# Top-k attention and a gated feed-forward on one core: score halves in one op, last keys of P.V in column halves, a retuned order

## The chip, the cores and the metric

One core of one Trainium2 chip runs the whole program in one launch. The metric is device microseconds (us) of an execution. The engines are called as the profile calls them: PE (TensorE, with PEld for its weight loads), DVE (VectorE), ACT (ScalarE), POOL (GpSimd) and SP (SyncE, which issues the DMAs). PE's clock has two levels here, 1.2 and 2.4 GHz; the profile gives the granted share of the higher one.

## What is computed

```python
def _attn_ref(q, k, v):                       # q, k, v: (4, 8, 576, 64)
    scores = scale * np.matmul(q, k.transpose(0, 1, 3, 2))
    kth = np.partition(scores, -32, axis=-1)[..., -32:-31]
    scores = np.where(scores >= kth, scores, -1e9)
    attn = np.exp(scores - np.max(scores, axis=-1, keepdims=True))
    attn = attn / (np.sum(attn, axis=-1, keepdims=True) + 1e-09)
    return np.matmul(attn, v)

def _moe_ref(x, w_gate, w_val, w_out, rms_g): # x: (2304, 512), 1536 hidden
    rms = np.sqrt(np.mean(x * x, axis=-1, keepdims=True) + 1e-06)
    xn = x / rms * rms_g
    g = xn @ w_gate
    silu = g * (1.0 / (1.0 + np.exp(-g)))
    return silu * (xn @ w_val) @ w_out
```

The three weights arrive as 64-bit floats; the kernel cuts them down on the chip.

## The kernel before

**Attention** goes in 72 steps. A step handles two heads (`e` = 0, 1) for 128 queries. Its scores (128 x 576 for each head) come in two key halves of 288. Each half is one PE op of six matmuls: `qh·kh`, `ql·kh` and `qh·kl` (values split into a high and a low part), each for both heads, with 64 rows of the array for each head (L513 to L525). An op writes two PSUM banks, one for each head. ACT copies each bank into the slot `sp` (L528). DVE then finds the 32nd largest score: minimum and maximum of the two halves (L501, L502, which read half 0 straight from its bank and half 1 from `sp`), one MAX8 over the minima (L503), and four MAX8 (L506) with three MATCH_REPLACE8 between them (L508). POOL makes the thresholds (L535), ACT and POOL mask, ACT takes the exponential (L539 to L541), PE transposes the nine 128-key blocks (L564), ACT copies them to `pt` and `ptt` (L566), and PE multiplies with `v` (P.V, L575 to L580). In P.V the head's 512 first keys go in matmuls on 64 columns of the array, one column half for each head, side by side; the 64 last keys of both heads go ahead of them in one matmul on all 128 columns (`ptt`, `vt[:, 512:640]`).

**The feed-forward** comes in units: after 256 tokens (after 128 at the start), their output is transposed and normalised (L624 to L665), then each of 12 blocks m (six in a 128-token unit) runs 24 gate and value matmuls into one bank (L697 to L706), ACT's tanh (L708), products on POOL (L711, L712) or on DVE (L714), the product with the value half (L715), a split, and the output matmuls (`wo`, L731 to L736).

**The weights** are read in the first part: 36 pieces (12 each of `w_gate`, `w_val`, `w_out`), each a DMA of 512 KB into one of two raw buffers. A piece is cut down in three DVE instructions (L356 to L358), or, where `PR["HV"]` has the weight's bit, at half its value in two DVE instructions, an ACT Sign and a POOL add (L351 to L354). A POOL subtraction makes the low part of either (L362).

**The order** of every engine's instructions is written by a planner, `_Plan`: each op has an engine, a duration, a priority (`pri`, with offsets from the table `PR`) and its PSUM banks. `place` walks through time, takes for a free engine the ready op of the best priority whose banks are free, and the ops are emitted by their planned start. On the chip each engine then follows that fixed order and waits with semaphores. Banks belong to groups: four in `a` (scores, transposes, P.V, weights), two in `g` (gates), two in `o` (outputs). The key `("turn", 0)` keeps a half-0 score op behind L502 of the step before.

Of the kernel before, what the change touches and what calls it, by code (L numbers as in the profile page):

```python
# [34 lines left out]
)  # L35

# [14 lines left out]
class _Plan:  # L51
# [10 lines left out]
    def add(self, eng, dur, fn, r=(), w=(), bank=None, pri=0.0, nbytes=0, sh=False):  # L62
        o = _Op()
        banks = () if bank is None else bank if isinstance(bank, tuple) else (bank,)
        o.eng, o.dur, o.fn, o.pri, o.banks, o.nbytes, o.sh = eng, dur, fn, pri, banks, nbytes, sh
        o.succ, o.pred = [], []
        deps = {}
        for key in r:
            p = self.writer.get(key)
            if p is not None:  # L70
                deps[id(p)] = (p, True)
            self.readers.setdefault(key, []).append(o)
        for key in w:
            for x in self.readers.get(key, ()):
                if x is not o:
                    deps.setdefault(id(x), (x, False))
            p = self.writer.get(key)
            if p is not None:
                deps[id(p)] = (p, True)
            self.writer[key] = o  # L80
            self.readers[key] = []
        for b in banks:
            if b.last is None:
                b.first = o
            else:
                deps.setdefault(id(b.last), (b.last, False))
            b.last = o
        for p, raw in deps.values():
            p.succ.append((len(self.ops), raw))
            o.pred.append((p.index, raw))  # L90
        o.index = len(self.ops)
        self.ops.append(o)
        return o

    def place(self, key, back=False):
# [14 lines left out]
        busy, win, warm = {}, 0, False  # L110
# [4 lines left out]
        while left:  # L115
            for e in range(5):
# [109 lines left out]
def tile_topk_attention_moe(  # L226
# [30 lines left out]
    NS, NK, NV, NQ, NPT, NWO, NQR = 4, 4, 2, 3, 3, 2, 2  # L257
# [4 lines left out]
    krawt = sb("krawt", [64, 2, 2, D])  # L262
# [45 lines left out]
    def build(exact):  # L308


        plan = _Plan({"a": banks[0:4], "g": banks[4:6], "o": banks[6:8]})
# [82 lines left out]
        def prep_k(b, pair, pri):  # L394
# [4 lines left out]
            dma(krawt[:, g], k[b, h0:h0 + 2, 512:576].rearrange("h s d -> s h d"), 32768, (), (("krawt", g),), pri - 2)  # L399
# [3 lines left out]
            tail = _Bank("a")  # L403
            add(PE, 0.12, lambda: nc.tensor.transpose(tail.tile[:, 0:64], krawt[:, g].rearrange("p h d -> p (h d)"), ident[0:64, 0:64]), r=(("krawt", g),), w=(("kh", s, 1), ("kl", s, 1)), bank=tail, pri=ko)
            ends = [t[s].rearrange("p (n c) -> p n c", c=64)[:, 0:10:9, :] for t in (kh, kl)]

            def twice():
                return tail.tile[:, 0:64].unsqueeze(1).to_broadcast([128, 2, 64])
            add(ACT, 0.19, lambda: nc.scalar.copy(ends[0], twice()), w=(("kh", s, 1),), bank=tail, pri=ko)
            add(DVE, 0.2, lambda: nc.vector.tensor_tensor(ends[1], twice(), ends[0].bitcast(F32), op=ALU.subtract), r=(("kh", s, 1),), w=(("kl", s, 1),), bank=tail, pri=ko)  # L410
# [10 lines left out]
        def vkeys(s):  # L421
            return ("vt", s, 0), ("vt", s, 1)
# [59 lines left out]
        def topk(i, e, bank, pri):  # L482
# [18 lines left out]
            add(DVE, 0.365, lambda: nc.vector.tensor_tensor(mn[:, e, :], bank.tile[:, 0:half], b, op=ALU.min), r=bk, w=(nk,), bank=bank, pri=pri)  # L501
            add(DVE, 0.365, lambda: nc.vector.tensor_tensor(row[:, 0:half], bank.tile[:, 0:half], b, op=ALU.max), r=bk + (("turn", 0),), w=(mk,), bank=bank, pri=pri)  # L502
            add(DVE, 0.385, lambda: nc.vector.max(row[:, half:half + 8], mn[:, e, :]), r=(nk,), w=(mk,), pri=pri)  # L503
            for n in range(4):
                o8 = row[:, rounds[n]]
                add(DVE, 0.388, lambda o8=o8: nc.vector.max(o8, row[:, 0:half + 8]), w=(mk,), pri=pri + 0.1 * n)  # L506
                if n < 3:
                    add(DVE, 0.446, lambda o8=o8: nc.vector.match_replace(row[:, 0:half + 8], o8, row[:, 0:half + 8], NEG), w=(mk,), pri=pri + 0.1 * n)  # L508

        def attend(i, cols, qs, sums, pri):  # L510
# [3 lines left out]
            for half in (1, 0):  # L514
                bank = tuple(_Bank("a") for e in range(2))

                def sm(bank=bank, half=half):
                    terms = [(col, pair, qq, kk) for pair, col in cols for qq, kk in ((qh, kh), (ql, kh), (qh, kl))]
# [51 lines left out]
        def attend_out(i, j, pair, vs, pri):  # L570
# [4 lines left out]
            def pv():  # L575
                mm(bank.tile[:, 0:128], vv[:, 512:640], pc, True, False)
# [3 lines left out]
            add(PE, 1.3, pv, r=(ck, ak, bk) + vkeys(vs), w=(("xv", j, pair),), bank=bank, pri=pri)  # L580
            add(ACT, 0.245, lambda: nc.scalar.copy(xv[:, pair, j * 128:(j + 1) * 128], bank.tile[:, 0:128]), w=(("xv", j, pair),), bank=bank, pri=pri + PR["EV"])

        def attend_out_tail(i, b, half, vs, rslot, pri):
# [21 lines left out]
            add(PE, 1.64, pv, r=(ck, ak, bk) + vkeys(vs[0]) + vkeys(vs[1]), w=(("xvt", 0), ("xvt", 1)), bank=bank, pri=pri)  # L605
# [8 lines left out]
        def feed_forward(u, js, xs, xkeys, rslot, stores, pri, last=False):  # L614
# [57 lines left out]
            for m in range(FC // per):  # L672
# [19 lines left out]
                gb = _Bank("g")  # L692
# [187 lines left out]
```

## Time and profile before

| | |
|---|---|
| median of 3 runs | 917.86 us (914.8 to 918.97) |
| profiled execution, its own time | 917.72 us |
| its span, first to last instruction | 915.8 us |
| mean granted PE clock | 0.955 |

The span is what the profile sees; the run's time is 1.9 us longer. "Busy" of an engine is the union of its instructions' records, which overlap in the pipelines; how long an instruction holds its engine is seen better in the distance between two starts.

### The profile page before, as it was taken

To read this page: it belongs to the slowest core of one execution; us is meant where nothing else is said; L and a number is where in the kernel's file an instruction comes from. 1 tells how busy PE (TensorE), PEld (TensorE's weight loads), DVE (VectorE), ACT (ScalarE), POOL (GpSimd) and SP (SyncE) were. 2 spreads that over 40 slices of the span, in tenths; PEclk is the share of its full clock that TensorE was granted. 3 is DMA by queue.
4 is the path that set the end of the run, shared out by engine and by line. 5 is a ranking of instruction groups with operands and counts; after the bars stand their busy time and mean duration, and the time that the engine had idled before them with its cause. 6 is when DMAs were issued, how large, how long until landed. Compare 5 with 4: busy or idle time off the path is not lost.

```text
span 915.8 us, 19289 instructions
## 1 busy us (share of the span) xinstructions
PE 837.1 (91%) x6618; PEld 714.5 (78%) x6618; DVE 727.7 (79%) x2272; ACT 621.7 (68%) x1549; POOL 517.8 (57%) x742
## 2 busy tenths in 40 slices
PE   5578776799899989999999989999999999999996
PEld 3456555678788858888888778889888988889995
DVE  5999998987798899965999889866898869694211
ACT  5766766787677887776778777766687667755311
POOL 6458998957665555667557544474653444434211
PEclk9976977999999999999999989999999999999999
DMA  9143675454643232224333313145332242332432
GB/s 242 53 137 109 214 229 207 155 175 132 193 121 99 97 93 79 100 83 133 125 100 106 125 61 112 47 135 170 102 115 89 88 158 99 96 110 80 132 134 97
DMA packets 86651, 112.89 MB, mean 123 GB/s; under 512 B 50832, under 2 KB 64144, under 8 KB 86544
## 3 DMA queue, kind: packets, MB, share of 16 engines
q1 hardware_dynamic: 86544, 111.57, 38.6%
q8 instruction: 54, 0.88, 0.4%
q14 instruction: 53, 0.43, 0.2%
HBM read 100.53 MB, written 11.01 MB: 122 GB/s over the span
## 4 chain that ended last, share of the span: by engine, by line
PE 75%; DVE 11%; DMA 5%; ACT 4%; POOL 2%; issue 1%; SPq 0%; POOLq 0%; DVEq 0%; ACTq 0%
PE bank L315 65%; PE bank L564 7%; DVE mx L506 3%; DVE mx L508 3%; DMA kraw<-in_moe_w_val_dram 2%; DMA kraw<-in_moe_w_out_dram 1%; PE bank L443 1%; ACT rr L539 1%; DVE mn L501 1%; PE bank L415 1%; PE bank L624 1%; DVE mx L502 1%; PE bank L659 1%; DVE mx L503 1%; ACT sp L541 1%
## 5 line engine op out<-in xcount | busy, mean ns | idle before, releaser
L506 DVE MAX8 mx<-mx 128x8 f32<-128x296 f32 x576 | 241.6, 455 | 0.0
L540 POOL TENSOR_TENSOR sp<-sp,rr 128x576 f32<-128x576 f32 x144 | 183.9, 1289 | 76.6 <-ACT rr L539 71.1
L508 DVE MATCH_REPLACE8 mx<-mx 128x296 f32<-128x296 f32 x432 | 191.9, 451 | 0.0
L315 PE MATMUL bank<-wo,hh 128*128 128x512 f32 x432 | 149.0, 426 | 3.3 <-DMA wo<-wosc 1.4
L727 POOL TENSOR_TENSOR hl<-tg,hh 128x256 fp32r<-128x256 f32 x108 | 79.4, 737 | 116.9 <-ACT hh L726 102.4
L564 PE MATMUL bank<-ident,sp 128*128 128x128 f32 x648 | 108.6, 293 | 26.5 <-ACT sp L541 6.2
L528 ACT COPY sp<-bank 128x288 f32<-128x288 f32 x288 | 101.2, 405 | 36.6 <-PE bank L315 34.7
L541 ACT ACTIVATE sp<-sp,bt 128x576 f32<-128x576 f32 x144 | 112.7, 783 | 11.7 <-POOL sp L540 11.3
L539 ACT ACTIVATE rr<-sp,bt 128x576 bf16<-128x576 f32 x144 | 108.0, 779 | 12.2 <-POOL bt L535 12.1
L315 PE MATMUL bank<-xth,wgh 128*128 128x256 f32 x384 | 116.3, 303 | 0.0
L564 PEld LDWEIGHTS bank<-ident,sp 128*128 128x128 f32 x648 | 79.6, 148 | 46.7 <-ACT sp L541 7.6
L315 PE MATMUL bank<-xth,wvh 128*128 128x256 f32 x384 | 112.4, 293 | 0.0
L566 ACT COPY pt<-bank 128x512 f32<-128x512 f32 x144 | 84.7, 590 | 37.7 <-PE bank L564 33.7
L315 PE MATMUL bank<-xtl,wgh 128*128 128x256 f32 x384 | 107.7, 281 | 0.0
L315 PE MATMUL bank<-xth,wgl 128*128 128x256 f32 x384 | 107.7, 280 | 0.0
L315 PE MATMUL bank<-xth,wvl 128*128 128x256 f32 x384 | 107.3, 279 | 0.0
L315 PE MATMUL bank<-xtl,wvh 128*128 128x256 f32 x384 | 107.2, 279 | 0.0
L708 ACT ACTIVATE tg<-bank 128x256 f32<-128x256 f32 x108 | 41.5, 385 | 78.7 <-PE bank L315 77.2
L714 DVE SCALAR_TENSOR_TENSOR tg<-tg,bank 128x256 f32<-128x256 f32 x76 | 31.6, 415 | 74.8 <-ACT tg L708 74.3
L501 DVE TENSOR_TENSOR mn<-bank,sp 128x288 f32<-128x288 f32 x144 | 60.7, 448 | 35.7 <-ACT sp L528 35.3
L315 PE MATMUL bank<-kh,qh 64*128 64x288 f32 x320 | 73.5, 396 | 15.5 <-DVE mx L502 5.1
L315 PE MATMUL bank<-wo,hl 128*128 128x512 f32 x216 | 86.6, 401 | 0.2
(151 smaller groups left out, 2076.2 us busy)
## 6 DMA issues: line engine op xcount, KB each, us to landing
wo<-wosc SPq DMA_DIRECT2D x108, 512.0 KB, 3.3
vt<-in_v_dram SPq DMA_DIRECT2D x52, 256.0 KB, 3.0
xvt<-in_moe_w_gate_dram SPq DMA_DIRECT2D x12, 512.0 KB, 4.2
wosc<-wo SPq DMA_DIRECT2D x12, 512.0 KB, 3.6
kraw<-in_k_dram SPq DMA_DIRECT2D x32, 128.0 KB, 3.2
kraw<-in_moe_w_val_dram SPq DMA_DIRECT2D x8, 512.0 KB, 3.8
qraw<-in_q_dram SPq DMA_DIRECT2D x56, 64.0 KB, 2.4
out_dram<-osb SPq DMA_DIRECT2D x14, 256.0 KB, 2.4
```

The lines of the kernel that those rows point to most:

```text
L315: nc.tensor.matmul(o, l, r, start=start, stop=stop)
L501: add(DVE, 0.365, lambda: nc.vector.tensor_tensor(mn[:, e, :], bank.tile[:, 0:half], b, op=ALU.min), r=bk, w=(nk,), bank=bank, pri=pri)
L506: add(DVE, 0.388, lambda o8=o8: nc.vector.max(o8, row[:, 0:half + 8]), w=(mk,), pri=pri + 0.1 * n)
L508: add(DVE, 0.446, lambda o8=o8: nc.vector.match_replace(row[:, 0:half + 8], o8, row[:, 0:half + 8], NEG), w=(mk,), pri=pri + 0.1 * n)
L528: add(ACT, 0.32, lambda b=bank[e], c0=c0: nc.scalar.copy(sp[s][:, c0:c0 + 288], b.tile[:, 0:288]), w=(("sp", s, e, half),), bank=bank[e], ...
L539: add(ACT, 0.7, lambda e=e, tl=tl: nc.scalar.activation(rr[e], tl, AF.Relu, bias=bt[t][:, e, 2:3], scale=-BIG), r=(("bt", t),) + spkeys(i, ...
L540: add(POOL, 1.27, lambda e=e, tl=tl: nc.gpsimd.tensor_tensor(tl, tl, rr[e], op=ALU.subtract), r=(("rr", e),), w=spkeys(i, e), pri=pri + PR ...
L541: add(ACT, 0.8, lambda e=e, tl=tl: nc.scalar.activation(tl, tl, AF.Exp, bias=bt[t][:, e, 1:2], scale=SCALE, accum_out=sums(e)[0]), r=(("bt ...
L564: nc.tensor.transpose(bank.tile[:, c * 128:(c + 1) * 128], sp[s][:, c0 + c * 128:c0 + (c + 1) * 128], ident)
L566: add(ACT, 0.228 if n == 1 else 0.507, lambda dst=dst, bank=bank, n=n: nc.scalar.copy(dst[:, 0:n * 128], bank.tile[:, 0:n * 128]), w=(key, ...
L708: add(ACT, 0.325, lambda gb=gb, hs=hs: nc.scalar.activation(th[hs], gb.tile[:, 0:256], AF.Tanh, scale=1.0 if halves[0] else 0.5), w=(("th" ...
L727: add(POOL, 0.75, lambda hs=hs: nc.gpsimd.tensor_tensor(hl[hs], th[hs], hh[hs].bitcast(F32), op=ALU.subtract), r=(("th", hs), ("hh", hs)), ...
```

## The change

- Both score halves of both heads become one PE op of 12 matmuls and four banks; the `turn` key now holds for the whole op.
- The last keys in P.V go in two column halves, so that a P.V op has one tile shape from its first matmul to its last.
- The transposes of the last 64 keys of K are made for two pairs at once, on the whole array.
- The gates' bank group is dissolved: `a` has six banks.
- The planner adds `SWITCH` to a PE op whose mode (1: row halves, 2: column halves, 0: the rest) differs from that of the op before.
- `sp` has five slots for four, `pt` four for three.
- `HV` 6 to 7: `w_gate`'s twelve pieces go the way of L351 to L354 too. `Z0` 2 to 0: no block takes the POOL way of L710 to L712 any more, all take L714.
- The other numbers of `PR` and some planned durations change.

```diff
-    HV=6, SU=1, ZU=5, F1=2, FX0=-3, FS0=0.5, FD0=-2, Z0=2, QN=0, FE=-8, EV=-1, SO=-2.5, WP1=0.5, WI=-4, FO=-0.5, FS=0.8, ZP=0, KO=-3, WP0=1, FB=3.5, AO=-0.9, FX=-30, QO=-3, TB=0.1, WO=-4, SM=0,
+    HV=7, SU=1, ZU=6, F1=5.02, FX0=-3.08, FS0=0.39, FD0=-2.4, Z0=0, QN=0, FE=-9.01, EV=-2.13, SO=-2.7, WP1=0.21, WI=-6.69, FO=2.17, FS=0.8, ZP=0, KO=-4.26, WP0=1.0, FB=3.5, AO=0.79, FX=-16.28, QO=-3, TB=0.35, WO=-1.76, SM=1.12,
+SWITCH = 0.2
...
+                    if o.mode != mode:
+                        dur, mode = dur + SWITCH, o.mode
...
-    NS, NK, NV, NQ, NPT, NWO, NQR = 4, 4, 2, 3, 3, 2, 2
+    NS, NK, NV, NQ, NPT, NWO, NQR = 5, 4, 2, 3, 4, 2, 2
...
-        plan = _Plan({"a": banks[0:4], "g": banks[4:6], "o": banks[6:8]})
+        plan = _Plan({"a": banks[0:6], "o": banks[6:8]})
...
+            if g == 0:
...
+                add(PE, 0.11, lambda: nc.tensor.transpose(tail.tile[:, 0:128], krawt.rearrange("p h d -> p (h d)"), ident), r=(("krawt", 0), ("krawt", 1)), w=tuple((n, t, 1) for n in ("kh", "kl") for t in two), bank=tail, pri=ko)
...
-            for half in (1, 0):
-                bank = tuple(_Bank("a") for e in range(2))
...
+            bank = {(half, e): _Bank("a") for half in (1, 0) for e in range(2)}
...
+            def sm():
+                for half in (1, 0):
                     for n, (col, pair, qq, kk) in enumerate(terms):
                         for e in range(2):
                             es = slice(64 * e, 64 * e + 64)
                             c0 = 64 * (1 - e) + half * 288
-                            mm(bank[e].tile[:, 0:288], qq[qs][es, col, :], kk[pair % NK][es, c0:c0 + 288], n == 0, n == len(terms) - 1)
...
+                            mm(bank[half, e].tile[:, 0:288], qq[qs][es, col, :], kk[pair % NK][es, c0:c0 + 288], n == 0, n == len(terms) - 1)
+            kk = tuple((n, pair % NK, z) for n in ("kh", "kl") for pair, _ in cols for z in range(2))
+            add(PE, 0.8 * len(cols), sm, r=(("qh", qs), ("ql", qs)) + kk, w=spkeys(i, 0, 1) + ((("turn", 0),) if not exact else ()), bank=tuple(bank.values()), pri=pri + PR["SO"], mode=1)
...
             def pv():
-                mm(bank.tile[:, 0:128], vv[:, 512:640], pc, True, False)
+                for e in range(2):
+                    mm(bank.tile[64 * e:64 * e + 64, 0:128], vv[:, 512 + 64 * e:576 + 64 * e], pc, True, False)
...
-                gb = _Bank("g")
+                gb = _Bank("a")
```

PE in the feed-forward of a 256-token unit, with the scores of attention step 41 (`kh`, `kl`, `qh`, `ql`) between gate matmuls (`xth`, `xtl` with `wgh`, `wgl`). Before, the first half of that step's scores:

```order
L315 MATMUL bank_68<-xth,wgl 128x256
L315 MATMUL bank_65<-kh_79,qh_94 128x288
L315 MATMUL bank_66<-kh_79,qh_94 128x288
L315 MATMUL bank_65<-kh_79,ql_97 128x288
L315 MATMUL bank_66<-kh_79,ql_97 128x288
L315 MATMUL bank_65<-kl_83,qh_94 128x288
L315 MATMUL bank_66<-kl_83,qh_94 128x288
L315 MATMUL bank_68<-xth,wgh 128x256
L315 MATMUL bank_68<-xtl,wgh 128x256
```

The same step's scores on PE in the changed kernel:

```order
L321 MATMUL bank_64<-kh_79,qh_94 128x288
L321 MATMUL bank_66<-kh_79,qh_94 128x288
L321 MATMUL bank_64<-kh_79,ql_97 128x288
L321 MATMUL bank_66<-kh_79,ql_97 128x288
L321 MATMUL bank_64<-kl_83,qh_94 128x288
L321 MATMUL bank_66<-kl_83,qh_94 128x288
L321 MATMUL bank_67<-kh_79,qh_94 128x288
L321 MATMUL bank_65<-kh_79,qh_94 128x288
L321 MATMUL bank_67<-kh_79,ql_97 128x288
L321 MATMUL bank_65<-kh_79,ql_97 128x288
L321 MATMUL bank_67<-kl_83,qh_94 128x288
L321 MATMUL bank_65<-kl_83,qh_94 128x288
```

Before, four more gate matmuls and then the second half follow these rows; now the halves stand together, with a gate block of 24 matmuls behind them.

PE at the first P.V of the program, before (`ptt` holds the last keys of both heads, `pt` the others):

```order
L564 MATMUL bank_66<-ident,sp_98 128x128 x9
L315 MATMUL bank_66<-ptt_118,vt_87 128x128
L315 MATMUL bank_66<-pt_115,vt_87 64x128
L315 MATMUL bank_66<-pt_116,vt_87 64x128
L315 MATMUL bank_66<-pt_115,vt_87 64x128
```

And in the changed kernel:

```order
L575 MATMUL bank_64<-ident,sp_98 128x128 x4
L575 MATMUL bank_67<-ident,sp_98 128x128
L575 MATMUL bank_68<-ident,sp_98 128x128 x4
L321 MATMUL bank_67<-ptt_120,vt_87 64x128 x2
L321 MATMUL bank_67<-pt_118,vt_87 64x128
```

One matmul on 128 columns has become two on 64; the tile shape still changes once ahead of the P.V and once behind it.

DVE at the start of the program, before (`kl` is the low part of the last keys of K, `xvt` and `tg` raw weights):

```order
L356 TENSOR_SCALAR bank_63<-xvt 128x512
L357 SCALAR_TENSOR_TENSOR bank_63<-xvt,bank_63 128x512
L358 SCALAR_TENSOR_TENSOR x_120<-xvt,bank_63 128x512
L351 TENSOR_SCALAR bank_65<-tg 128x512
L352 SCALAR_TENSOR_TENSOR osb<-tg,bank_65 128x512
L410 TENSOR_TENSOR kl_83<-bank_64,kh_79 128x2x64
```

And in the changed kernel:

```order
L420 TENSOR_TENSOR kl_83<-bank_64,kh_79 128x2x64
L420 TENSOR_TENSOR kl_84<-bank_64,kh_80 128x2x64
L357 TENSOR_SCALAR bank_66<-xvt 128x512
L358 SCALAR_TENSOR_TENSOR x_122<-xvt,bank_66 128x512
L357 TENSOR_SCALAR bank_65<-tg 128x512
L358 SCALAR_TENSOR_TENSOR osb<-tg,bank_65 128x512
L511 TENSOR_TENSOR mn<-bank_63,sp_98 128x288
```

K comes ahead of the weights now, a piece of `w_gate` takes two instructions in place of three, and the first step's search starts behind two pieces; before, four pieces stand ahead of it.

## Rows read from the trace of the kernel before

**Rows 1.** The page: busy time of each engine; the chain that ended last.

```profile
PE 837.1 (91%) x6618; PEld 714.5 (78%) x6618; DVE 727.7 (79%) x2272; ACT 621.7 (68%) x1549; POOL 517.8 (57%) x742
...
PE 75%; DVE 11%; DMA 5%; ACT 4%; POOL 2%; issue 1%; SPq 0%; POOLq 0%; DVEq 0%; ACTq 0%
```

**Rows 2.** Windows: length, busy PE, PEld, DVE, ACT, POOL, then clock, DMA.

```profile
100.00:125.00 25.00, 15.71 (x102) 11.96 (x101) 23.43 (x59) 18.06 (x42) 22.91 (x24) 0.91 0.78 247
...
0.00:175.00 175.00, 119.73 (x672) 88.78 (x673) 156.66 (x427) 119.46 (x276) 130.21 (x165) 0.81 0.55 173
175.00:321.00 146.00, 141.43 (x1230) 121.64 (x1229) 125.38 (x416) 113.40 (x296) 95.17 (x133) 1.00 0.43 133
321.00:346.00 25.00, 19.85 (x129) 14.12 (x127) 24.84 (x82) 20.74 (x53) 14.56 (x30) 0.93 0.32 100
...
519.00:540.00 21.00, 15.01 (x87) 11.70 (x87) 19.82 (x64) 17.34 (x43) 12.70 (x27) 0.76 0.33 108
540.00:854.00 314.00, 313.81 (x2657) 278.42 (x2656) 244.27 (x785) 209.37 (x524) 148.86 (x228) 1.00 0.33 104
854.00:916.00 62.00, 54.38 (x377) 49.39 (x375) 11.78 (x28) 12.71 (x30) 9.56 (x13) 0.97 0.38 129
```

**Rows 3.** Timeline of PE around half a step's scores: start, duration, instruction.

```profile
429.15 0.28 PE L315 MATMUL bank<-xth,wgl 128*128 128x256 f32 x1
429.36 0.40 PE L315 MATMUL bank<-kh,qh 64*128 64x288 f32 x2
429.60 0.29 PE L315 MATMUL bank<-kh,ql 64*128 64x288 f32 x2
429.73 0.29 PE L315 MATMUL bank<-kl,qh 64*128 64x288 f32 x2
429.96 0.39 PE L315 MATMUL bank<-xth,wgh 128*128 128x256 f32 x1
430.19 0.28 PE L315 MATMUL bank<-xtl,wgh 128*128 128x256 f32 x1
430.30 0.28 PE L315 MATMUL bank<-xth,wgl 128*128 128x256 f32 x1
```

**Rows 4.** Timeline of PE at a P.V and the transposes behind it.

```profile
395.15 0.38 PE L315 MATMUL bank<-ptt,vt 128*128 128x128 f32 x2
395.47 1.09 PE L315 MATMUL bank<-pt,vt 128*64 128x128 f32 x16
396.49 1.20 PE L564 MATMUL bank<-ident,sp 128*128 128x128 f32 x9
```

**Rows 5.** Groups of instructions by line and form: count, busy us, mean ns, idle before.

```profile
L315 PEld LDWEIGHTS bank<-pt,vt 128*64 128x64 f32 x1280 | 68.9, 145 | 9.3 <-issue 1.8
...
L714 DVE SCALAR_TENSOR_TENSOR tg<-tg,bank 128x256 f32<-128x256 f32 x76 | 31.6, 415 | 74.8 <-ACT tg L708 74.3
...
L712 POOL TENSOR_TENSOR tg<-tg 128x256 f32<-128x256 f32 x32 | 23.6, 736 | 1.1
...
L357 DVE SCALAR_TENSOR_TENSOR bank<-xvt,bank 128x512 uint32<-128x512 uint32 x12 | 8.3, 695 | 0.3
...
L354 POOL TENSOR_TENSOR x<-x,wo 128x512 int32<-128x512 int32 x5 | 6.5, 1291 | 0.0
```

**Rows 6.** The same view of DVE's first 175 us: two of these to a step.

```profile
L503 DVE MAX8 mx<-mn 128x8 f32<-128x288 f32 x26 | 11.0, 449 | 0.0
```

**Rows 7.** The waits: who waited for whom, us, times, longest.

```profile
DVE mn L501 <- ACT sp L528: 35.3, 23, 6.1
```

**Rows 8.** What the engine waited for ahead of instructions with K: us, times.

```profile
  DVE mx L502: 12.2, 13
```

**Rows 9.** The chain that ended last, at the start: start, us.

```profile
3.23 5.20 DMA kraw<-in_k_dram
8.56 1.10 PE bank L415 x4
```

**Rows 10.** Timeline of DVE: the first instruction of the first search.

```profile
18.58 0.46 DVE L501 TENSOR_TENSOR mn<-bank,sp 128x288 f32<-128x288 f32 x1 [2.27 <-ACT sp L528]
```

More of the change, by code (lines that the diff above doesn't have):

```diff
@@ L60, in __init__, with add @@
         self.bank_tail = {}
-    def add(self, eng, dur, fn, r=(), w=(), bank=None, pri=0.0, nbytes=0, sh=False):
+    def add(self, eng, dur, fn, r=(), w=(), bank=None, pri=0.0, nbytes=0, sh=False, mode=0):
         o = _Op()
         banks = () if bank is None else bank if isinstance(bank, tuple) else (bank,)
-        o.eng, o.dur, o.fn, o.pri, o.banks, o.nbytes, o.sh = eng, dur, fn, pri, banks, nbytes, sh
+        o.eng, o.dur, o.fn, o.pri, o.banks, o.nbytes, o.sh, o.mode = eng, dur, fn, pri, banks, nbytes, sh, mode
         o.succ, o.pred = [], []
@@ L109, in place @@
         dma_free = t = 0.0
-        busy, win, warm = {}, 0, False
+        busy, win, warm, mode = {}, 0, False, 0
         left = len(ops)
@@ L261, in tile_topk_attention_moe @@
     kraw = sb("kraw", [128, 2, 4, 2, D])
-    krawt = sb("krawt", [64, 2, 2, D])
+    krawt = sb("krawt", [128, 2, D])
     kh = [sb(f"kh{i}", [128, S + 64], F32R) for i in range(NK)]
@@ L402, in prep_k, with twice @@
             ko = pri + PR["KO"]
[L403 to L410, printed above, removed]
+            if g == 0:
+                for y in range(2):
+                    dma(krawt[64 * y:64 * y + 64], k[b, h0 + 2 * y:h0 + 2 * y + 2, 512:576].rearrange("h s d -> s h d"), 32768, (), (("krawt", y),), pri - 2)
+                tail = _Bank("a")
+                two = (s, s + 1)
+                add(PE, 0.11, lambda: nc.tensor.transpose(tail.tile[:, 0:128], krawt.rearrange("p h d -> p (h d)"), ident), r=(("krawt", 0), ("krawt", 1)), w=tuple((n, t, 1) for n in ("kh", "kl") for t in two), bank=tail, pri=ko)
+                for y, t in enumerate(two):
+                    ends = [n[t].rearrange("p (n c) -> p n c", c=64)[:, 0:10:9, :] for n in (kh, kl)]
+                    def twice(y=y):
+                        return tail.tile[:, 64 * y:64 * y + 64].unsqueeze(1).to_broadcast([128, 2, 64])
+                    add(ACT, 0.19, lambda ends=ends, twice=twice: nc.scalar.copy(ends[0], twice()), w=(("kh", t, 1),), bank=tail, pri=ko)
+                    add(DVE, 0.25, lambda ends=ends, twice=twice: nc.vector.tensor_tensor(ends[1], twice(), ends[0].bitcast(F32), op=ALU.subtract), r=(("kh", t, 1),), w=(("kl", t, 1),), bank=tail, pri=ko)
             bank, z = _Bank("a"), slot()
@@ L522, in sm @@
                             c0 = 64 * (1 - e) + half * 288
-                            mm(bank[e].tile[:, 0:288], qq[qs][es, col, :], kk[pair % NK][es, c0:c0 + 288], n == 0, n == len(terms) - 1)
-                kk = tuple((n, pair % NK, z) for n in ("kh", "kl") for pair, _ in cols for z in range(2))
-                add(PE, 0.42 * len(cols), sm, r=(("qh", qs), ("ql", qs)) + kk, w=tuple(("sp", s, e, half) for e in range(2)) + ((("turn", 0),) if half == 0 and not exact else ()), bank=bank, pri=pri + PR["SO"])
+                            mm(bank[half, e].tile[:, 0:288], qq[qs][es, col, :], kk[pair % NK][es, c0:c0 + 288], n == 0, n == len(terms) - 1)
+            kk = tuple((n, pair % NK, z) for n in ("kh", "kl") for pair, _ in cols for z in range(2))
+            add(PE, 0.8 * len(cols), sm, r=(("qh", qs), ("ql", qs)) + kk, w=spkeys(i, 0, 1) + ((("turn", 0),) if not exact else ()), bank=tuple(bank.values()), pri=pri + PR["SO"], mode=1)
+            for half in (1, 0):
                 for e in range(2):
                     c0 = e * S + half * 288
-                    add(ACT, 0.32, lambda b=bank[e], c0=c0: nc.scalar.copy(sp[s][:, c0:c0 + 288], b.tile[:, 0:288]), w=(("sp", s, e, half),), bank=bank[e], pri=pri + PR["SO"])
+                    add(ACT, 0.32, lambda b=bank[half, e], c0=c0: nc.scalar.copy(sp[s][:, c0:c0 + 288], b.tile[:, 0:288]), w=(("sp", s, e, half),), bank=bank[half, e], pri=pri + PR["SO"])
             for e in range(2):
-                topk(i, e, bank[e], pri + PR["TB"] * e)
+                topk(i, e, bank[0, e], pri + PR["TB"] * e)
             if exact:
@@ L596, in pv @@
                 for z in range(2):
-                    mm(bank.tile[:, z * 64:z * 64 + 64], vt[vs[z]][:, 512:640], pc[:, z * 64:z * 64 + 64], z == 0, False)
+                    for e in range(2):
+                        mm(bank.tile[64 * e:64 * e + 64, z * 64:z * 64 + 64], vt[vs[z]][:, 512 + 64 * e:576 + 64 * e], pc[:, z * 64:z * 64 + 64], z == 0, False)
                 for z in range(2):
@@ L604, in pv @@
                             )
-            add(PE, 1.64, pv, r=(ck, ak, bk) + vkeys(vs[0]) + vkeys(vs[1]), w=(("xvt", 0), ("xvt", 1)), bank=bank, pri=pri)
+            add(PE, 1.15, pv, r=(ck, ak, bk) + vkeys(vs[0]) + vkeys(vs[1]), w=(("xvt", 0), ("xvt", 1)), bank=bank, pri=pri, mode=2)
             add(
```

16 lines of the change are left out of this document (7 added, 9 removed).

## Prediction

> **What bounds the kernel now.** I read the page's busy times and chain first, then the windows, then PE's timeline. PE is busy 91% of the span and holds 75% of the chain that ended last; DVE follows with 79% and 11% [rows 1]. The average hides stages, so the windows come next [rows 2]. Up to 175 us PE is busy for 119.7 us at a mean clock of 0.81, and DVE for 156.7 of 175: this stage belongs to DVE, with POOL close behind it (22.9 of 25 us from 100 to 125). From there PE is the bound: 313.8 of 314 us from 540 to 854, and nearly so in the windows around it. Two short stretches are the exception: from 321 to 346 PE is busy for 19.9 of 25 us while DVE has 24.8, and from 519 to 540 for 15.0 of 21 with DVE at 19.8, at granted clocks of 0.93 and 0.76. There PE has run out of feed-forward work and waits for the search. The last 62 us are PE's alone (DVE 11.8). So what takes time off PE's stream behind 175 us comes off the end, and DVE's work counts in the first stage and those two stretches.
>
> **What a change of tile shape costs.** The timeline of PE around half a step's scores shows it [rows 3]. Gate matmuls start 0.11 to 0.12 us apart (430.19 to 430.30) and pairs of score matmuls 0.13 (429.60 to 429.73). Into the row halves it takes 0.21 to the first pair (429.15 to 429.36) and 0.24 to the next: 0.09 and 0.11 too much. Back out it takes 0.23 and 0.23: 0.10 and 0.11 too much. So one change costs 0.20 us of PE's stream. P.V shows the same: 0.32 us from `ptt` to `pt` for a matmul on all columns (two records for one fp32 matmul) [rows 4].
>
> **PE's changes of shape.** By PE's order there are 395 before and 272 now. The score halves make most of it: 121 visits to the row shape become 72, since each step comes in one piece, and the 13 visits for K's last keys vanish because they are turned on the whole array. Where scores stand directly behind a P.V, the `ptt` matmul no longer adds a shape of its own. Up to the end of step 13's scores (the first stage: 26 L503 rows, two to a step [rows 6]) it is 59 against 42, hidden under DVE. Behind that 336 against 230: 106 × 0.20 = **21.2 us**, all on PE's stream.
>
> **PE's work.** Twelve score matmuls cost what twice six did. A P.V took 0.32 for `ptt` and 1.02 for the rest [rows 4]; without the halves of changes in them that is 0.22 and 0.82, so 0.205 for a pair of column halves (four such pairs). `ptt` as a fifth pair saves 0.02 × 64 = 1 us; the eight ops of the last queries I take alike. Sixteen transposes of K's last keys become eight, 0.13 each (nine in 1.20): 1 us. Together **2 us**. If the halves ran one behind the other, `ptt` would cost 0.2 more for 72 ops, 15 us; but the 16 records in 1.02 us already show them side by side.
>
> The Trainium skill ("TensorE: Matmul & The Clock Gate", Part 3, the mechanism) says that a weight load overlaps running matmuls only if it is for other rows of the array, which would speak against splitting the last keys: column halves share their rows. Here the trace disagrees: 16 loads of 145 ns [rows 5] would make 2.3 us, and the 16 matmuls started within 1.02 [rows 4]. By that rule two more loads for each of 64 ops would add up to 19 us and eat the gain of the shapes.
>
> **The first stage.** Twelve `w_gate` pieces lose one DVE instruction of 0.70 each (8.3 us less) and gain a POOL addition of 1.29 (15.5 us more) [rows 5] and a Sign on idle ACT. In exchange POOL loses some ten products of 0.74 here (in the run all 64, half of them L711, half L712), and DVE gets some five more L714 of 0.42. The sum is DVE -6 us, POOL +8, of which a third falls where POOL has room. K is also asked for ahead of the weights. Before, the DMA of K ended on the chain at 8.4, its transposes began at 8.6 [rows 9] and the first search at 18.6 [rows 10]; I expect it some 6 us sooner, but the pieces that filled this time come later. Bounds: 10 us less, where DVE sets the pace all along; 8 more, if POOL does. Both are near their limit, so I take **3 us less**.
>
> **The two stretches.** Their PE idle time is 5.2 + 6.0 us, and the clock took some 1.7 and 5.0 more (the shares missing from 0.93 and 0.76) [rows 2]: 18 us could be had. DVE's order tells where they lie: three steps go by without a gate product, between steps 25 and 28 and between 45 and 48. In the new order the longest such gap is one, from step 17 to 20. I credit one stretch in part: **5 us less**; bounds 15 less and 5 more.
>
> **DVE, ACT and POOL behind the first stage.** The L714 that replace the POOL way cost DVE 32 × 0.42 = 13.3 us in the run, weights give 8.3 back: 728 becomes 733. This hides under PE while PE is the bound; without cover it is 24 × 0.42 = 10 us behind the first stage. ACT and POOL lose work. More slots of `sp` and `pt` cost nothing.
>
> **The new wait.** An op that needs four of six banks, and by `turn` the minima and maxima of the step before, can hold PE's queue: gates, outputs and transposes behind it all wait, and through them ACT and POOL. Before, PE and its loads waited for L502 12.2 us in 13 places ahead of work on K [rows 8]. I take **4 us more**; bounds 0 (the order has room) and 15 (the 12.2 us once more, a fifth longer for the faster pace).
>
> **Sum.** -21.2 - 2 - 3 - 5 + 4 = -27 us. The profiled run took 917.7 (span 915.8), 0.1 under the median: **890.5 us**, -3%.
>
> **The rivals.**
>
> *Banks and scores late, gain halved.* Every step's search needs ACT's copies; DVE waited for them 35.3 us in 23 places, up to 6.1 [rows 7]. The four-bank op gives the search nothing until it has run in one piece, some 0.4 us of six matmuls and the copies later than a half did. For it: two of the six banks are held until L502 at any time. Against it: DVE has 188 idle us over the span [rows 1]. With the bank wait at its bound of 15 and the stretches unchanged: 917.7 - 21 - 2 - 3 + 15 = 907. The Trainium skill ("TensorEngine Tiling (Array Packing)", PSUM Bottleneck) has the same concern: tiling speeds up the array, not the emptying of PSUM. Here ACT, which empties these banks, is at 68% [rows 1]. Chance 0.16.
>
> *Slower: the search becomes the bound.* Ahead of 854 us DVE is idle for 188 - 50 = 138 us (62 - 11.8 in the last window [rows 2]). If the score op comes later at each of 72 steps, DVE pays it each time: 1.9 us a step use up the idle time at the present end. From there each further 0.1 is 7 us: at 2.2 us a step 138 becomes 158, 938 us. Against it: a half-0 op already stood behind the same `turn`. Chance 0.05.
>
> *No change.* The time off PE returns as waiting for DVE, step by step, because orders were fitted to each other: 917 ± 4. The 0.2 us idle from 540 to 854 [rows 2] speak against it: DVE had 70 us to spare there. Chance 0.06.
>
> *POOL stretches the first stage.* With 8 more there and nothing from the start, 11 above the forecast: 901. Chance 0.10.
>
> *Better.* Both stretches go and the early start counts: 890.5 - 10 - 7 = 874. Chance 0.13.
>
> My own case has 0.50, and with its small terms it spans 882 to 900.
>
> **How the numbers follow.** About 0.5% (4.6 us) is what a measurement of this kernel can tell from no change. Of the better case half lies under 875, and of the cases above 909 there are "no change", "slower" and a part of the halved gain, together some 0.13. So 875 to 909 leaves 0.2 out. Faster by over 0.5% (under 913.3) are my case, the halved gain, POOL and the better one: 0.89; within 0.5% 0.06; slower 0.05.
>
> **What the profile of the changed kernel should show.** PE's timeline: twelve score matmuls in one piece, 0.8 us and two changes around them, with gates in whole blocks. PE's instructions: no transposes of 64 rows, `ptt` on 64 columns. Windows: PE without idle time from about 175 us to its end, total busy time some 20 us less. DVE's first L501 around 12 us, the last weight piece not later than 171. If waits of score matmuls for L502's counterpart (L512) or for the copies exceed 25 us, the halved gain holds; if a window of 100 us shows DVE busy throughout and PE idle, the slower rival does. I'd be wrong about the main term if changes of shape fall as counted and PE's pace between them does not.

## The result and the profile after

| | before | after |
|---|---|---|
| median | 917.93 us of 4 runs | **878.29 us** of 4 runs (876.06 to 879.04) |
| profiled execution, its own time | 917.72 us | 879.04 us |
| its span | 915.8 us | 876.8 us |

The ratio is 0.957, with a 95% interval of 0.954 to 0.9599: 39 us faster, where 27 were forecast. The time lies inside the range (875 to 909) but at its lower end, under my own case (882 to 900), toward the "better" rival. So the direction was right, and some term was too small.

The page of the changed kernel, busy time of each engine and the chain that ended last, as in [rows 1]:

```profile
PE 798.7 (91%) x6770; PEld 701.6 (80%) x6770; DVE 726.7 (83%) x2292; ACT 617.6 (70%) x1529; POOL 488.1 (56%) x690
...
PE 77%; DVE 10%; DMA 6%; ACT 3%; POOL 2%; issue 1%; SPq 0%; DVEq 0%; ACTq 0%; POOLq 0%
```

PE is still the bound at the same 91%, but of a shorter span: it is busy 38.4 us less. (Its records rose from 6618 to 6770: the split of the last keys makes 160 more, the transposes of K's last keys 8 fewer.) I had forecast some 20 less. A busy time holds two things, the work and the clock at which it ran, so the windows come next: window, length, busy PE, PEld, DVE, ACT and POOL, then granted clock, DMA share, GB/s. The changed kernel:

```profile
0.00:240.00 240.00, 173.72 (x1247) 141.61 (x1248) 216.06 (x635) 180.90 (x428) 183.68 (x232) 0.83 0.56 175
300.00:360.00 60.00, 58.45 (x525) 51.11 (x525) 59.05 (x192) 47.82 (x121) 31.18 (x52) 1.00 0.31 97
480.00:540.00 60.00, 59.69 (x535) 52.49 (x532) 58.42 (x188) 48.66 (x124) 31.73 (x53) 1.00 0.37 115
240.00:876.80 636.80, 624.94 (x5525) 560.03 (x5523) 510.68 (x1658) 436.75 (x1102) 304.42 (x459) 1.00 0.36 111
```

The same windows of the kernel before (the two of 60 us hold the stretches of [rows 2]):

```profile
0.00:240.00 240.00, 180.15 (x1195) 139.28 (x1196) 210.00 (x603) 170.68 (x410) 174.42 (x230) 0.86 0.54 170
300.00:360.00 60.00, 54.76 (x441) 45.09 (x441) 57.77 (x192) 48.52 (x125) 36.34 (x57) 0.97 0.27 84
480.00:540.00 60.00, 54.01 (x412) 44.83 (x412) 54.70 (x180) 48.27 (x123) 37.11 (x57) 0.92 0.35 108
240.00:915.80 675.80, 656.97 (x5425) 575.22 (x5424) 517.74 (x1669) 450.99 (x1140) 343.43 (x513) 0.99 0.34 107
```

The reader is to see three things. First, behind 240 us, where PE is the bound, its busy time falls by 32.0 us and its idle time from 18.8 to 11.9. The mark is a time and not a place in the work, so that it says nothing of the first part that all 39.0 us (675.8 against 636.8) lie behind it. What PE had done by then differs little: the trace has 18 score and six output matmuls more ahead of it and eight gate matmuls fewer, by their pitches about 2 us of work. The search is two steps further (20 for 18), and PE is idle for longer (66.3 us for 59.9), at a clock of 0.83 for 0.86. Second, both stretches of [rows 2] in which PE had idle time are gone: 5.24 + 5.99 idle us in the two windows have become 1.55 + 0.31, and the clock stays at 1.00 where it was 0.97 and 0.92, which is 1.8 + 4.8 us of clock. Third, DVE is no faster (726.7 us busy for 727.7), and it holds little less of the chain (10% for 11%).

PE's timeline at one score op of the changed kernel (start, duration, instruction), to be held against [rows 3]:

```profile
343.31 0.27 PE L321 MATMUL bank<-xth,wvl 128*128 128x256 f32 x1
343.52 0.41 PE L321 MATMUL bank<-kh,qh 64*128 64x288 f32 x2
343.75 0.30 PE L321 MATMUL bank<-kh,ql 64*128 64x288 f32 x2
343.89 0.30 PE L321 MATMUL bank<-kl,qh 64*128 64x288 f32 x2
344.02 0.30 PE L321 MATMUL bank<-kh,qh 64*128 64x288 f32 x2
344.15 0.31 PE L321 MATMUL bank<-kh,ql 64*128 64x288 f32 x2
344.29 0.31 PE L321 MATMUL bank<-kl,qh 64*128 64x288 f32 x2
344.52 0.50 PE L321 MATMUL bank<-wo,hh 128*128 128x512 f32 x1
```

The second half follows the first at the plain pitch of 0.13 to 0.14 (343.89, 344.02). The slow places stand only at the ends: 0.21 and 0.23 going in, 0.23 coming out. Before, each half paid them.

What PE waited for, summed over the run: the two largest causes, and then the largest wait of a weight load for L512, the counterpart of L502 (us, times, longest):

```profile
PE bank L575 <- ACT sp L552: 25.5, 16, 4.1
PE bank L321 <- DMA wo<-wosc: 8.4, 5, 3.5
...
PEld bank L321 <- DVE mx L512: 0.7, 2, 0.4
```

Of the 25.5 us for the exponential (L552), 24.5 lie ahead of 240 us, where PE is not the bound. No matmul waited for L512, and weight loads waited 0.9 us for it in all. Before, matmuls of L315 waited 5.1 us for L502 and their weight loads 7.1, for the most part at the same places; the 12.2 us of [rows 8] are the two added up. DVE's first search begins at 12.20 us (18.58 before [rows 10]), and 175 us still hold the maxima of 13 steps, as in [rows 6], though the 13th comes at 166.9 us for 174.4. First DVE's timeline, then its group of that stretch:

```profile
12.20 0.46 DVE L511 TENSOR_TENSOR mn<-bank,sp 128x288 f32<-128x288 f32 x1 [1.25 <-ACT sp L539]
...
L513 DVE MAX8 mx<-mn 128x8 f32<-128x288 f32 x26 | 10.9, 449 | 0.0
```

### The profile page after: what moved, and what is told of

Same layout as the page of the kernel before. It is cut to its first block, busy times and chain, and to the rows that moved or that the text cites. A ratio compares the mean times of both kernels' runs of the same rounds, so it can differ in the third digit from the quotient of the medians.

```text
span 876.8 us, 19543 instructions
## 1 busy us (share of the span) xinstructions
PE 798.7 (91%) x6770; PEld 701.6 (80%) x6770; DVE 726.7 (83%) x2292; ACT 617.6 (70%) x1529; POOL 488.1 (56%) x690
## 4 chain that ended last, share of the span: by engine, by line
PE 77%; DVE 10%; DMA 6%; ACT 3%; POOL 2%; issue 1%; SPq 0%; DVEq 0%; ACTq 0%; POOLq 0%
PE bank L321 66%; PE bank L575 8%; DVE mx L516 2%; DVE mx L518 2%; DMA wo<-wosc 2%; DMA xvt<-in_moe_w_gate_dram 2%; PE bank L425 1%; DVE bank L357 1%; PE bank L453 1%; DMA kraw<-in_k_dram 1%; DMA xvt<-in_moe_w_out_dram 1%; DVE mx L513 1%; ACT sp L552 1%; PE bank L672 1%; PE bank L637 1%
## 5 line engine op out<-in xcount | busy, mean ns | idle before, releaser
L575 PE MATMUL bank<-ident,sp 128*128 128x128 f32 x648 | 100.1, 286 | 29.1 <-ACT sp L552 25.5
L552 ACT ACTIVATE sp<-sp,bt 128x576 f32<-128x576 f32 x144 | 113.1, 787 | 13.7 <-POOL sp L551 13.0
L539 ACT COPY sp<-bank 128x288 f32<-128x288 f32 x288 | 97.1, 409 | 24.2 <-PE bank L321 23.4
L321 PE MATMUL bank<-xth,wgh 128*128 128x256 f32 x384 | 113.5, 296 | 0.2 <-ACT xv L593 0.2
L575 PEld LDWEIGHTS bank<-ident,sp 128*128 128x128 f32 x648 | 77.6, 146 | 43.8 <-ACT sp L552 30.6
L321 PE MATMUL bank<-xth,wvh 128*128 128x256 f32 x384 | 110.5, 288 | 0.0
L727 DVE SCALAR_TENSOR_TENSOR tg<-tg,bank 128x256 f32<-128x256 f32 x108 | 44.3, 411 | 68.5 <-ACT tg L721 68.3
L321 PEld LDWEIGHTS bank<-wo,hh 128*128 128x128 f32 x432 | 71.9, 194 | 25.0 <-DMA wo<-wosc 8.3
L546 POOL TENSOR_TENSOR bt<-mx,cst 128x6 f32<-128x6 f32 x72 | 14.4, 200 | 125.3 <-DVE mx L516 124.3
```

Source lines behind the costliest of these rows:

```text
L321: nc.tensor.matmul(o, l, r, start=start, stop=stop)
L539: add(ACT, 0.32, lambda b=bank[half, e], c0=c0: nc.scalar.copy(sp[s][:, c0:c0 + 288], b.tile[:, 0:288]), w=(("sp", s, e, half),), bank=ban ...
L552: add(ACT, 0.8, lambda e=e, tl=tl: nc.scalar.activation(tl, tl, AF.Exp, bias=bt[t][:, e, 1:2], scale=SCALE, accum_out=sums(e)[0]), r=(("bt ...
L575: nc.tensor.transpose(bank.tile[:, c * 128:(c + 1) * 128], sp[s][:, c0 + c * 128:c0 + (c + 1) * 128], ident)
L727: add(DVE, 0.365, lambda gb=gb, hs=hs: nc.vector.scalar_tensor_tensor(th[hs], th[hs], 1.0, gb.tile[:, 0:256], op0=ALU.add, op1=ALU.mult), ...
```

## The experiments

Two theories stood against each other. **Shapes**: what counts is the number of changes of tile shape on PE. **Order**: the gain is in the order that the planner writes (slots, banks, table, durations), and shapes matter little. Twelve kernels tell them apart. "Changes" are PE's changes of shape, in all and behind step 13: before 395 and 336, after 272 and 230. The kernel before ran again beside each set: 917.5 to 917.7 us.

**1 and 2. The same order with more changes.** Both kernels put one more transpose into each score op, into columns that nothing reads. In the one it stands between the halves, in the other at the op's front. PE does the same work in both.

```diff
+                    if half == 0:
+                        nc.tensor.transpose(bank[0, 0].tile[:, 384:512], ident, ident)
```

> The changed kernel with one 128x128 transpose of the identity put between the two halves of each score op, into columns of the bank that nothing reads; order and everything else as they were. It leaves the row shape and comes back: 416 changes of shape in place of 272 (114 more than in the twin run behind step 13). Shapes theory (a change costs 0.20 us of PE's stream and PE is the bound): 114 x 0.20 = 23 us above the twin, about 909 us. Order theory (most of the gain came from the new order, PE waits for DVE anyway): less than 8 us above the twin.

```diff
             def sm():
+                nc.tensor.transpose(bank[0, 0].tile[:, 384:512], ident, ident)
```

> The twin: the same 72 transposes, at the front of the score op, where the whole-array shape mostly stands already: 277 changes of shape. Both theories: the work of the transposes alone, 64 of them behind the first stage at 0.11 us, and 5 changes: 8 us, 886 us.

Measured: in the middle 904.19 us (901.22 to 908.6; ratio to before 0.985, 0.9812 to 0.9887) with 416 and 348 changes; at the front 884.45 (880.04 to 884.94; 0.9629, 0.9588 to 0.967) with 277 and 234. Between them 114 changes behind step 13 cost 19.7 us: 0.17 us each, where 0.20 had been read from the timeline. The two intervals leave some 5 us either way, which is 0.04 a change, so 0.20 isn't ruled out. Set against the changed kernel, the front version is 6.2 us longer, about what 59 transposes behind step 13 at 0.11 make (6.5). PE's timeline of the first shows where the time goes:

```profile
409.15 0.40 PE L321 MATMUL bank<-kh,qh 64*128 64x288 f32 x2
409.39 0.29 PE L321 MATMUL bank<-kh,ql 64*128 64x288 f32 x2
409.52 0.29 PE L321 MATMUL bank<-kl,qh 64*128 64x288 f32 x2
409.74 0.33 PE L530 MATMUL bank<-ident 128*128 128x128 f32 x1
410.00 0.40 PE L321 MATMUL bank<-kh,qh 64*128 64x288 f32 x2
410.24 0.29 PE L321 MATMUL bank<-kh,ql 64*128 64x288 f32 x2
```

From the last pair of the first half to the second pair of the next (409.52 to 410.24) it is 0.72. Two plain pitches of 0.13 and the transpose's 0.11 make 0.37 of it; 0.35 is left for two changes. So changes of shape cost what the rows say, on an unchanged order. The Trainium skill ("TensorEngine Tiling (Array Packing)", Key Properties) says that a change of tiling mode drains TensorE. The trace agrees as far as it goes: every change costs time, 0.17 us here, though no row shows the drain itself.

**3. The last keys on all columns again**, order kept:

```diff
-                for e in range(2):
-                    mm(bank.tile[64 * e:64 * e + 64, 0:128], vv[:, 512 + 64 * e:576 + 64 * e], pc, True, False)
+                mm(bank.tile[:, 0:128], vv[:, 512:640], pc, True, False)
```

> The changed kernel with the last keys of the P.V back in one matmul on all 128 columns; order kept. 281 changes of shape in place of 272. Shapes theory: 9 x 0.20 and 64 x 0.02 us, 3 us above the changed kernel (881). Rival (weight loads of column halves are not hidden): two loads fewer for each of 64 ops, up to 19 us below it.

Measured: 881.78 (878.07 to 882.44; 0.9607, 0.9567 to 0.9647), with 281 and 239 changes. That is 3.5 us over the changed kernel, with intervals that overlap. The same P.V on PE's timeline, first in the changed kernel:

```profile
387.23 0.28 PE L321 MATMUL bank<-xth,wgl 128*128 128x256 f32 x1
387.44 0.44 PE L321 MATMUL bank<-ptt,vt 128*64 128x128 f32 x4
387.71 1.04 PE L321 MATMUL bank<-pt,vt 128*64 128x128 f32 x16
388.68 0.66 PE L425 MATMUL bank<-ident,kraw 128*128 128x128 f32 x4
```

and with the last keys on all columns:

```profile
388.52 0.28 PE L321 MATMUL bank<-xth,wgl 128*128 128x256 f32 x1
388.63 0.39 PE L321 MATMUL bank<-ptt,vt 128*128 128x128 f32 x2
388.95 1.09 PE L321 MATMUL bank<-pt,vt 128*64 128x128 f32 x16
389.97 0.66 PE L425 MATMUL bank<-ident,kraw 128*128 128x128 f32 x4
```

From the gate matmul to the transposes it takes 1.45 us in both: the change is only paid ahead of `ptt` or behind it. So between gates the split brings nothing; what is left of it is the nine changes next to score ops, some 1.5 us. Nor does the split cost anything near the 19 us of two more loads for each op that the prediction weighed: then this kernel would be up to 19 us under the changed one, and the intervals leave at most 3 (0.9599 - 0.9567). The rule behind these 19 us, of the Trainium skill ("TensorE: Matmul & The Clock Gate", Part 3, the mechanism), is that a weight load overlaps running matmuls only for other rows of the array; this run doesn't bear it out.

**4. The halves in two ops again**, everything else as changed, order planned anew:

```diff
-            bank = {(half, e): _Bank("a") for half in (1, 0) for e in range(2)}
+            for half in (1, 0):
+                bank = tuple(_Bank("a") for e in range(2))
...
+                add(PE, 0.4 * len(cols), sm, r=(("qh", qs), ("ql", qs)) + kk, w=tuple(("sp", s, e, half) for e in range(2)) + ((("turn", 0),) if half == 0 and not exact else ()), bank=bank, pri=pri + PR["SO"], mode=1)
```

> The changed kernel with the score halves in two ops of two banks each again; the planner orders anew with the same table: 340 changes of shape, 58 more than now behind step 13. Shapes theory: 58 x 0.20 = 12 us above the changed kernel, 890 us. Rival (the op of four banks makes PE wait): the wait goes, and the time comes out no higher than 878 us.

Measured: 885.9 (883.65 to 886.43; 0.9653, 0.9618 to 0.9688) with 340 and 288 changes. So with 58 changes more behind step 13 it is 7.6 us longer, 0.13 for each; the order is a new one, and PE's idle time behind 240 us is 2.0 us shorter in it (9.9), so the price is not as clean as the one above. The count does not go back to 336, because PE's 13 visits to the row shape for K's last keys stay away and because the planner still puts some halves side by side: 110 visits for scores, where it was 121 before and 72 in the changed kernel. The edit in the diff's centre is thus worth 8 of the 39 us. The wait that the rival named is not there to be saved: PE is busy 60.00 of 60 us from 300 to 360 here, and the time went up.

**5 to 7. The table.** Fifth: the changed kernel with the whole old `PR`. Sixth: with the old offsets, but `HV=7`, `ZU=6`, `Z0=0`. Seventh: the kernel before with the new `PR`.

```diff
-    HV=7, SU=1, ZU=6, F1=5.02, FX0=-3.08, FS0=0.39, FD0=-2.4, Z0=0, QN=0, FE=-9.01, EV=-2.13, SO=-2.7, WP1=0.21, WI=-6.69,
...
+    HV=6, SU=1, ZU=5, F1=2, FX0=-3, FS0=0.5, FD0=-2, Z0=2, QN=0, FE=-8, EV=-1, SO=-2.5, WP1=0.5, WI=-4,
...
```

> The changed kernel with the whole old table of numbers (so w_gate in three DVE instructions, two of three gate blocks over POOL, old offsets): 271 changes of shape. Shapes theory: it keeps the 21 + 2 us of shapes and P.V and loses the start and the stretches: 895 us. Order theory (the new numbers and ways bring more than half of the 39 us): 900 to 918 us.

> The changed kernel with the old offsets, but with the new ways of w_gate and of the gate blocks (HV 7, ZU 6, Z0 0): 267 changes of shape. If the ways make the difference to the run with the whole old table, it is near 880 us; if the offsets do, it is where that run is, 895 us in the shapes theory.

> The kernel before with the new table (ways and offsets), score halves apart, old banks, old P.V: 388 changes of shape. Shapes theory: the shapes stay (at most 1 us less), a few us from the start: 905 to 918 us. Order theory: under 900 us.

Measured: 884.84 (883.85 to 888.11; 0.9642, 0.9605 to 0.9679); 888.87 (885.51 to 890.34; 0.9683, 0.964 to 0.9727); 917.24 over ten runs (914.71 to 920.92; 1.0004, 0.9983 to 1.0026). The table is worth 6.6 us on the changed kernel and nothing on the old one. Both theories had the fifth slower than it came out (895; 900 to 918), and the sixth is near neither of its two values: it isn't clearly apart from the fifth, so the new ways of `w_gate` and of the gates show no gain by themselves. (The old table sends 32 of the 108 gate blocks over POOL, not two of three: `Z0` holds for the first units only.) In the fifth, PE had done less by 240 us, 1183 records for 1247, while its idle time behind that grew by 1.1 us only. The table isn't what removed the stretches: with the old table they stay away (PE busy 58.98 and 60.00 in the windows from 300 and 480), and on the kernel before with the new table they remain (52.78 and 56.82).

**8. The old slots**, all else as changed:

```diff
-    NS, NK, NV, NQ, NPT, NWO, NQR = 5, 4, 2, 3, 4, 2, 2
+    NS, NK, NV, NQ, NPT, NWO, NQR = 4, 4, 2, 3, 3, 2, 2
```

> The changed kernel with four slots of sp and three of pt: 272 changes of shape, new order by the planner. Prediction's view (slots cost and bring nothing): 878 us. Rival (the fifth slot is what lets PE run ahead and removed the stretches in which DVE set the pace): 885 to 895 us, with idle time of PE in the middle of the run.

Measured: 905.41 (903.58 to 906.14; 0.9872, 0.9835 to 0.991), 27 us over the changed kernel with about the same number of changes (272 and 231), and slower than either forecast. Its windows:

```profile
300.00:360.00 60.00, 51.72 (x446) 43.20 (x445) 56.61 (x187) 45.45 (x116) 28.42 (x48) 0.94 0.25 76
480.00:540.00 60.00, 56.54 (x501) 48.16 (x500) 59.31 (x194) 48.28 (x123) 30.63 (x52) 1.00 0.29 91
720.00:780.00 60.00, 51.67 (x399) 42.81 (x399) 51.79 (x167) 39.66 (x101) 26.80 (x45) 1.00 0.38 112
```

The stretches are back, and a third one (720 to 780) has joined them. The waits of PE and of its loads for L512 are back as well, with the same op on the same six banks:

```profile
PEld bank L321 <- DVE mx L512: 6.9, 8, 2.1
PE bank L321 <- DVE mx L512: 4.9, 5, 1.9
```

So two numbers in a line of declarations, which I had put at nothing, carry more than the score op does. Which of the two it is, only the order tells, and no run: planned with four slots of `sp` and four of `pt`, the instructions of every engine follow each other as in the changed kernel (slot numbers aside); with five and three they follow each other as in this one. By that it is the fourth slot of `pt`. The kernel's text says why it can matter: a step's transposed weights take two slots of `pt`, and K and Q go through it too when they are split (L391 in the kernel before), so that three slots don't hold what two steps need.

**9 and 10. The slot on the kernel before**: alone, and together with one group of six banks.

```diff
-    NS, NK, NV, NQ, NPT, NWO, NQR = 4, 4, 2, 3, 3, 2, 2
+    NS, NK, NV, NQ, NPT, NWO, NQR = 4, 4, 2, 3, 4, 2, 2
```

> The kernel before with a fourth slot of pt and nothing else; the planner orders anew: 398 changes of shape, and the two places at which three steps go by without a gate product (steps 25 to 28, 45 to 48) are gone from DVE's order. Slot theory (the fourth slot lets the transposes of a step run ahead of the P.V of the one before, and that removes the stretches in which PE waits for DVE): 895 to 903 us. Rival (the slot only pays together with the four-bank op): 912 to 920 us.

```diff
-        plan = _Plan({"a": banks[0:4], "g": banks[4:6], "o": banks[6:8]})
+        plan = _Plan({"a": banks[0:6], "o": banks[6:8]})
...
-                gb = _Bank("g")
+                gb = _Bank("a")
```

> The same with the gates' banks in the common group of six: 375 changes of shape, 23 fewer than in the run with the slot alone. If banks matter only through the shapes: 4 us below that run. If they take waits away too: 8 us or more below it.

Measured: alone 916.2 over ten runs (914.11 to 918.07; 0.9987, 0.997 to 1.0004), no difference; with six banks 897.32 (895.77 to 898.12; 0.9781, 0.9751 to 0.9811), 20 us faster with the old scores, the old P.V and the old table. Its changes of shape are 316 behind step 13, 20 fewer than before (3.4 us at 0.17); the other 17 fit the stretches, whose idle time and lost clock in the two windows are 17.5 us less than before. Its windows:

```profile
300.00:360.00 60.00, 60.00 (x512) 52.26 (x512) 55.29 (x180) 47.98 (x125) 38.53 (x62) 1.00 0.35 110
480.00:540.00 60.00, 59.66 (x504) 51.30 (x501) 55.24 (x182) 47.32 (x124) 34.15 (x56) 1.00 0.34 106
240.00:894.90 654.90, 645.42 (x5444) 571.22 (x5442) 508.08 (x1643) 444.42 (x1129) 340.20 (x508) 1.00 0.35 108
```

PE's idle time behind 240 us halves, from 18.8 to 9.5. With the slot alone the stretches shrink (56.64 and 58.21 busy), but the time comes back in the first part:

```profile
0.00:240.00 240.00, 181.81 (x1150) 142.23 (x1151) 210.50 (x605) 169.53 (x406) 173.95 (x229) 0.81 0.55 169
```

There are 45 PE records fewer in it than before (x1195), at a clock of 0.81 for 0.86. Why the planner fills that part worse here stays open. Six banks without the fourth slot were not run, so how the 20 us divide between slot and banks stays open too.

**11. A fifth slot of `pt`** on the changed kernel:

```diff
-    NS, NK, NV, NQ, NPT, NWO, NQR = 5, 4, 2, 3, 4, 2, 2
+    NS, NK, NV, NQ, NPT, NWO, NQR = 5, 4, 2, 3, 5, 2, 2
```

> The changed kernel with five slots of pt: 264 changes of shape, 6 fewer behind step 13. If slots still bind: 870 us or less. If four are enough: 877 to 880 us (6 x 0.17 = 1 us from the shapes).

Measured: 880.82 (878.93 to 881.06; 0.9596, 0.9567 to 0.9625). It brings nothing more: with four the stretches are gone already.

**12. The planner without the cost of a change**:

```diff
-SWITCH = 0.2
+SWITCH = 0.0
```

> The changed kernel with the planner's SWITCH at 0: 276 changes of shape, 5 more behind step 13, and one stretch of 2.5 steps without a gate product (45 to 47.5). If the planned cost matters only through the shapes: 879 us. If the better timing of the plan is what keeps the stretches away: 885 us or more.

Measured: 901.27 (900.25 to 903.56; 0.9821, 0.9793 to 0.9849), 23 us over the changed kernel, with only 5 changes more behind step 13 (235), which is 1 us. Its windows:

```profile
300.00:360.00 60.00, 54.02 (x493) 46.43 (x493) 55.95 (x186) 46.55 (x120) 29.34 (x48) 1.00 0.29 89
480.00:540.00 60.00, 54.32 (x453) 47.41 (x452) 55.20 (x179) 44.92 (x111) 29.21 (x47) 0.94 0.32 96
240.00:901.50 661.50, 638.33 (x5588) 569.93 (x5586) 521.49 (x1684) 444.38 (x1116) 310.50 (x465) 0.99 0.35 107
```

PE is idle for 23.2 us behind 240, twice as long as in the changed kernel: 11.3 of the 23. The rest is clock (0.94 in the window from 480 to 540) and work that PE had not done by 240 us (1184 records for 1247). So the number does not pay by fewer changes: without it the planner writes an order in which PE waits. That this comes of taking PE for faster than it is, and that it is PE's feed-forward work which the plan then spends too early, is argued, not shown. No version ran faster than the changed kernel.

So neither theory holds alone. Changes of shape are worth some 18 us; the stretches, which hang on the order, are the next largest part.

## Why the prediction was off, by its own steps

**The changes of shape (-21.2): right, a little too large.** The count is that of PE's order, and the price held within its error (experiments 1 and 2). With 0.17 for 0.20 the 106 changes are 18 us.

**PE's work (-2): not resolved.** At the P.V above the split saves nothing; the fewer changes next to it are in the 106 already. Any remainder is under the 3.5 us of experiment 3.

**The two stretches (-5): the step that failed.** I sized them rightly, as idle time and clock worth 18 us, and then credited "one stretch in part", because I looked for their cause in DVE's gate products and wrote that "more slots of `sp` and `pt` cost nothing": true, but I gave them no gain either. I also took both for waits for the search. The first is: from 321 to 346 us the chain that ended last lies on DVE, 85% of it in the search (L501 to L508). From 519 to 540 it runs over ACT and PE with nothing of the search in it, and PE's longest wait there is for ACT's copy of Q into `pt` (at 533 us):

```profile
PE bank L659 <- ACT pt L391: 3.0, 1, 3.0
```

Both stretches went. By the two windows that is 9.4 idle us and 6.6 of clock, 16; by PE's idle time of the whole part behind 240 (6.9 less) and the same clock, 13.5. The bound that I gave was 15. Experiments 8, 10 and 12 show what they hang on: the slots, a slot together with the common banks, and the planner's cost. It is neither the table that I had compared (5 and 7) nor the score op (they are gone in 4 and 10, with halves apart).

**The new wait (+4): next to nothing.** Of the wait for the maxima 0.9 us of weight loads are left. My price was too high from the start, since most of the 12.2 us were the same waits counted twice, of matmuls (5.1) and of their loads (7.1). That six banks in common make up for an op that takes four isn't shown: with the old slots the same op on the same banks waits again (experiment 8).

**The first stage (-3): not shown.** The first search came when forecast, but the last weight piece didn't: I had it not later than 171 us. POOL's timeline (start, duration) has it at 178.47, in the kernel before at 187.97:

```profile
178.47 1.29 POOL L368 TENSOR_TENSOR wo<-qrt,wo 128x512 fp32r<-128x512 f32 x1
...
187.97 1.29 POOL L362 TENSOR_TENSOR wo<-qrt,wo 128x512 fp32r<-128x512 f32 x1
```

The search gained two steps by 240 us, but where PE is the bound only PE's own work counts, and of that some 2 us more were done by then. That is what 12 of the 106 changes are worth, which lie between step 13 and this mark. So a gain of the stage itself is not seen, and no run isolates it.

**What is left.** Of PE's 32.0 us less behind 240 us, 16 are the 94 changes that lie there, 2 the work done sooner and 6.6 the clock; 7.4 are left that no run places. PE's work (-2) may be in them, and at 0.20 for a change 3 more would be shapes.

**The sum.** 18 shapes, 13.5 stretches and 7.4 that no run places make 39; the last is a remainder, so that the sum proves nothing by coming out. Nine of the twelve us by which I missed are the stretches, four the wait that didn't come, two the remainder against the 5 that I gave the start and PE's work, and the shapes took 3 back; each of these is good to about 3 us. My own case (882 to 900) missed. That the range held is owed to the chance that I left for "better", and it was luck that the shapes, being smaller, took 3 us of the miss back.

**The rivals.** "Gain halved" wanted waits of score matmuls of over 25 us for the copies or L512, and neither is among PE's larger waits; DVE's wait for the copies fell from 35.3 us in 23 places [rows 7] to 23.7 in 13. "The search becomes the bound" and "no change" found no place. "POOL stretches the first stage" had POOL right (143.2 us busy up to 175 for 130.2), but not its price. "Better" (874) named the stretches and was the nearest; it deserved more than 0.13, since all that stood against it was that I had not found their cause. Its other half, 7 us from the early start, is not seen.

## What to carry to other kernels

Where a planner writes the order, a buffer slot or a more exact duration is an edit to every engine's order: compare the whole order with and without it before putting it at nothing. Where one engine is the bound and yet waits in a few places, price these places in full (idle time and lost clock) and ask for each edit, the small ones too, whether it removes them. A cost read from one row can be tested on an unchanged order, by two kernels that do the same extra work, once inside the pair and once ahead of it.

## What the runs showed of the hardware that was not expected

- A change of tile shape costs 0.17 us (experiments 1 and 2), about half at the first matmul of the new shape and half at the one behind it (0.09 and 0.11 too much in [rows 3]), and which of two neighbours pays it does not matter: a P.V took 1.45 us from gate to transposes in either form.
- Short waits of PE can cost more than their length: in the window from 480 to 540 the kernel before lost 6.0 us idle and 4.8 to the granted clock (0.92, with stretches at 1.2 GHz in it). In the changed kernel that window is at 1.00. Not all idle time was paid twice: experiment 8 has 8.3 us of it from 720 to 780, at a clock of 1.00.
- Two changes that bring 1.5 us (the slot alone, no clear difference) or are free on the old kernel (the table, 1.0004) belong to a set that brings 39: with the planned order, the effects of edits did not add.
